# Strassen's seven products for the down projection of a retention and feed-forward kernel

## Chip, cores and metric

The kernel runs on one core of a Trainium2 chip. The metric is the device time of one execution in microseconds (us), the median of several runs.

## What is computed

The reference is a retention layer (attention without softmax, with a decay by distance) followed by a feed-forward layer with a sigmoid gelu. Cut to what matters:

```python
scores = scale * np.matmul(q, k.transpose(0, 1, 3, 2))      # 8 batches, 8 heads, 576 positions, 64 wide
Dmat = np.where(rel >= 0, gamma[:, None, None] ** rel[None, :, :], 0.0)
attn = np.matmul(scores * Dmat[None], v)
x = attn.transpose(0, 2, 1, 3).reshape(4608, 512)
h = x @ w_in                                                # 512 x 2048
g = h * (1.0 / (1.0 + np.exp(-1.702 * h)))
out = g @ w_out                                             # 2048 x 512, float32
```

## The kernel before

**Units and chunks.** The 4608 tokens are 36 units of 128 (NU). Of each nine units, four belong to one batch, four to the next, and the ninth holds the last 64 positions of both ("the third kind": units 8, 17, 26, 35). Four units make a chunk, 0 to 8 (NCH = 9). The hidden width of 2048 is 16 slices f of 128 (NF).

**Feed-forward of a chunk.** In the up phase, `up(c, f)` (L552) makes four 512-wide matmuls into bank psA or psB, by turns with f, and ScalarE writes gelu of that bank into gT (L561). Chunk 1 uses `up_group` (L565) instead: two slices f of half the tokens, 256 columns each. In the down phase, `down(c, r, s, b)` (L580) makes four 512-wide matmuls for unit r over slices 4s to 4s+3, and after s = 3 `finish_unit` copies the bank to osb on ScalarE (L592) and stores it from SP's queue (L598). psA and psB change with r. Chunk 8 takes its units as 3, 0, 1 and then 2 in two column parts.

**Attention of a pair of units.** `block(j)` (L642) treats units 2j and 2j+1. On TensorE: `inter` (L466, reads the cast states kv and the transposed queries), `values` (L512, reads the masked scores pm and the scaled vp), and between its two phases `ahead(j + 1)` (L620), the scores (L491) and state updates (L419) of the next pair. On VectorE: `x_out_pair` (L540) writes the input xT of the feed-forward; then, by `ahead_out(j + 1)` (L627), `scores_out` (L504) twice and `state_sum` (L432) four times, two for a pair with a unit of the third kind. On ScalarE: `state_cast` (L444), which turns the new states into bf16 for the next block's `inter`. The arguments `nxt` and `cast` leave out the next pair's part, or put the cast elsewhere and the sums ahead of the scores.

**Order.** The order of each engine's instructions is written out by hand: every call of `op` appends to its engine's stream, and waits are worked out from the names read and written. An engine runs its stream in that order, and an instruction that waits holds up all that stand behind it on its engine. In a chunk c of 2 to 7, blocks 2c+2 and 2c+3 stand in the down phase, behind (r, s) = (0, 0) and (2, 0). Chunk 1 has block 3 in its up phase, without the next pair's part, and blocks 4 and 5 in its down phase. `scale_v(m)` (L343, vp from the loaded v) stands at f = 0, 4, 8, 12 of the up phase. At the top of a chunk stand the DMA transposes of four units on SP (L389) and the loads of four later units on POOL (L660), which wait for those transposes.

**Chunk 0** has PE transposes, copies and blocks of its own between its matmuls; `load_wout` (L267) brings w_out in four parts. Before the first data are there, `warm` matmuls run on a zeroed part of gT.

Of the kernel before, what the change touches and what calls it, by code (L numbers as in the profile page):

```python
# [160 lines left out]
def bass_retnet_parallel__then__act_gelu_quick_kernel(  # L161
# [10 lines left out]
    with es:  # L172
# [10 lines left out]
        osb = [sb(f"osb{i}", [P, DM], FP32) for i in range(4)]  # L183
# [6 lines left out]
        gT = [sb(f"gT{i}", [P, NF, 512], BF16) for i in range(2)]  # L190
# [17 lines left out]
        op = pr.op  # L208

# [34 lines left out]
        def load_kq0(which):  # L244
            src = (k, q)[which]
            op("sp", lambda e: e.dma_start(
                osb[1 + which].ap().rearrange("p (h d) -> p h d", d=DH),
                src[0, :, 0:P, :].rearrange("h p d -> p h d")),
               writes=[f"osb{1 + which}_0"], dma=f"d_kq0f_{which}")

        def cast_kq0(which, eng):
            dst, src = kqn[0][:, which, :, :], osb[1 + which].ap().rearrange("p (h d) -> p h d", d=DH)
            if eng == "act":
                op("act", lambda e: e.activation(dst, src, AF.Copy),
                   reads=[f"osb{1 + which}_0"], writes=[f"kq0_{which}"])
            else:
                op("dve", lambda e: e.tensor_copy(dst, src),
                   reads=[f"osb{1 + which}_0"], writes=[f"kq0_{which}"])
# [293 lines left out]
        def up(c, f, lo=0, hi=4, b=None):  # L552
            b = b or "AB"[f % 2]
            n0, n1 = P * lo, P * hi
            for a in range(4):
# [6 lines left out]
                gT[c % 2][:, f, n0:n1], bank[b][:, n0:n1], AF.Gelu_apprx_sigmoid),  # L562
               reads=[b], writes=[f"g{c % 2}_{f}_{j}" for j in range(lo, hi)])

        def up_group(c, f0, nf, lo, hi, b):  # L565
            n = P * (hi - lo)
            for i in range(nf):
# [8 lines left out]
                gT[c % 2][:, f0 : f0 + nf, P * lo : P * hi],  # L576
                bank[b][:, 0 : n * nf].rearrange("p (f t) -> p f t", f=nf), AF.Gelu_apprx_sigmoid),
               reads=[b], writes=[f"g{c % 2}_{f}_{j}" for f in range(f0, f0 + nf) for j in range(lo, hi)])

        def down(c, r, s, b, n0=0, n1=DM):  # L580
            for f in range(4 * s, 4 * s + 4):
                op("pe", lambda e, f=f: e.matmul(  # L582
                    bank[b][:, 0 : n1 - n0], gT[c % 2][:, f, P * r : P * r + P], w_out_sb[:, f, n0:n1],
                    start=(f == 0), stop=(f == NF - 1)),
                   reads=[f"g{c % 2}_{f}_{r}", f"wout{f // 4}"], writes=[b])

        def down_out(c, r, b, n0=0, n1=DM, cp="act", eng="sp"):
            u = 4 * c + r
            i = u % 4
            src, dst = bank[b][:, 0 : n1 - n0], osb[i][:, n0:n1]  # L590
            if cp == "act":
                op("act", lambda e: e.activation(dst, src, AF.Copy), reads=[b], writes=[f"osb{i}_{n0}"])  # L592
            else:
                op("dve", lambda e: e.tensor_copy(dst, src), reads=[b], writes=[f"osb{i}_{n0}"])

            def f(e):
                return [
                    e.dma_start(out[S * bb + s0 : S * bb + s0 + n, n0:n1], osb[i][p0 : p0 + n, n0:n1])  # L598
                    for p0, n, bb, s0 in unit_rows(u)
                ]  # L600
            return op(eng, f, reads=[f"osb{i}_{n0}"], writes=[f"out{u}_{n0}"],
                      dma=f"d_o{i}_{n0}", ndma=len(unit_rows(u)))
# [24 lines left out]
        def ahead_out(j, cast=True):  # L627
            if 2 * j >= NU:
                return
            if cast:  # L630
                scores_out(2 * j, 2, 0)
                scores_out(2 * j, 2, 1)
            for u in (2 * j, 2 * j + 1):
                for a in range(2):
                    state_sum(u, a)
            if not cast:
                scores_out(2 * j, 2, 0)
                scores_out(2 * j, 2, 1)
            if cast:
                state_cast(2 * j, 2 * j + 2)  # L640

        def block(j, nxt=None, cast=True):  # L642
            started.clear()
# [11 lines left out]
            for hh in range(2):  # L655
                x_out_pair(j, hh)
            if nxt is None:
                ahead_out(j + 1, cast)
# [7 lines left out]
        last_store = {}  # L666

        def finish_unit(c, r, b, **kw):
            o = down_out(c, r, b, **kw)
            last_store[o.dma] = o  # L670

        def warm(n, b='A', w=512):
            for i in range(n):
                op("pe", lambda e: e.matmul(
                    bank[b][:, 0:w], gT[1][:, 0, 0:P], gT[1][:, 0, 0:w], skip_group_check=True),
                   reads=["warm"], writes=[b])

        def warm_quads(n):
            for i in range(n):
                r, c = i % 2, (i // 2) % 2  # L680
                op("pe", lambda e, r=r, c=c: e.matmul(
                    bank["AX"[r]][64 * c : 64 * c + 64, 0:64], gT[1][64 * r : 64 * r + 64, 0, 0:64],
                    gT[1][64 * r : 64 * r + 64, 0, 0:64], skip_group_check=True),
                   reads=["warm"], writes=["AX"[r]])

        def gelu_table():
            op("act", lambda e: e.activation(gT[1][:, 1, 0:4], gT[1][:, 0, 0:4], AF.Gelu_apprx_sigmoid),
               reads=["warm"], writes=["gelu_table"])

        def lead_in():  # L690
# [18 lines left out]
            op("dve", lambda e: e.memset(gT[1][:, 0, :], 0.0), writes=["warm"])  # L709
# [75 lines left out]
            def ahead45():  # L785
# [12 lines left out]
                (3, 1): lambda: block(2, lambda: None),  # L798
# [3 lines left out]
            for r, s in [(i % 2, i // 2) for i in range(8)] + [(i // 4, i % 4) for i in range(8, NF)]:  # L802
                down(0, r, s, "AB"[r % 2])
                if (r, s) in work:
                    work[r, s]()
                if s == 3:
                    finish_unit(0, r, "AB"[r % 2])

        def steady():
            for c in range(1, NCH):  # L810
# [8 lines left out]
                for u in range(4 * c + 10, 4 * c + 14):  # L819
                    load(u, after=[f"T{(4 * c + 9) % NQT}_0"])  # L820
                if c == 1:
                    for i in range(16):
                        f0, lo = 2 * (i % 8), 2 * (i // 8)
                        up_group(1, f0, 2, lo, lo + 2, "AB"[i % 2])
                        if i == 0:
                            ahead(3)
                            ahead_out(3, False)
# [4 lines left out]
                        if i == 5:  # L832
                            block(3, lambda: None)
                            scale_v(8)
                            scale_v(9)
                        if i == 8:
                            scale_v(10)
                            scale_v(11)
                else:
                    for f in range(NF):  # L840
# [3 lines left out]
                        if f % 4 == 0:  # L844
                            m = 4 * c + 6 + f // 4
                            if m < NU:
                                scale_v(m)
                if c == NCH - 1:
                    for r in (3, 0, 1):
                        b = "AB"[(r + 1) % 2]  # L850
# [87 lines left out]
```

## Time and profile before

| what | value |
|---|---|
| median of 3 runs | 295.31 us (295.15 to 295.53) |
| profiled execution, span | 293.4 us |
| VectorE busy | 99.7 us, 202 instructions |
| ScalarE busy | 133.7 us, 235 instructions |
| up phase of chunk 3 | 112.09 to 125.91 us |
| down phase of chunk 3, two blocks in it | 125.91 to 142.27 us |
| gelu of 128x512 (L561) | 597 ns, 120 times |
| copy of 128x512 out of a bank (L592) | 584 to 596 ns |
| scores_out of 128x512 (L506) | 679 to 680 ns |
| state_sum of 128x256 (L441) | 419 to 424 ns |
| state_cast of 128x1024 / 128x512 (L450) | 1057 / 627 ns |

All times are of one profiled execution, in microseconds from the start of its span. The median of the runs is of other executions, and also holds what lies around the span: 295.31 - 293.4 = 1.9 us. A matmul's own duration in the profile contains its way through the array; for the pace of a row of them, the step from one to the next is what counts, as the chain gives it. Engines are named PE (TensorE, with PEld for its weight loads), DVE (VectorE), ACT (ScalarE), POOL (GpSimd) and SP (SyncE).

### The profile page before, as it was taken

The page shows a single profiled execution, that of the slowest core. Times are in us where ns is not written, and L with a number is a line of the kernel's source. Part 1 is how long each engine was busy: PE and PEld are TensorE (multiplying, and loading weights), DVE is VectorE, ACT ScalarE, POOL GpSimd, SP SyncE. Part 2 cuts the span into 40 slices and gives each one's busy share as a digit, 9 for nine tenths or more (in the row PEclk, how much of TensorE's full clock was granted, in tenths as well). Part 3 has the DMA queues.
Part 4 walks back from the last instruction along what each step waited for, and adds up shares of the span by engine and source line. Part 5 has one row for each costly group of instructions (what it writes and reads, how often), then busy time and mean ns, then how long its engine had stood idle before and what let it go on. Part 6 is the DMA issues. An engine that isn't in the chain of part 4 may idle for free.

```text
span 293.4 us, 8059 instructions
## 1 busy us (share of the span) xinstructions
PE 287.7 (98%) x3650; PEld 141.2 (48%) x3650; DVE 99.7 (34%) x202; ACT 133.7 (46%) x235; POOL 110.2 (38%) x141
## 2 busy tenths in 40 slices
PE   8899999999999999999999999999999999999996
PEld 6575456775533553345334533454344434443344
DVE  5861056615650652054404360237013700410000
ACT  7466234661366135712672256324642365216611
POOL 9999798000960590292049103910170000000000
PEclk9999999999999999999999999999999999999999
DMA  9999999998999899799479935992692050111022
GB/s 172 175 211 206 209 231 249 235 120 213 125 236 115 98 230 227 93 161 200 133 106 153 188 108 113 178 182 80 137 142 71 20 131 2 38 72 38 0 65 78
DMA packets 116786, 40.63 MB, mean 139 GB/s; under 512 B 104080, under 2 KB 109968, under 8 KB 116752
## 3 DMA queue, kind: packets, MB, share of 16 engines
q0 software_dynamic: 79712, 22.82, 68.0%
q1 hardware_dynamic: 36896, 17.24, 24.8%
q8 instruction: 28, 0.46, 0.7%
q10 hardware_dynamic: 144, 0.07, 0.1%
q14 instruction: 6, 0.05, 0.0%
HBM read 36.70 MB, written 9.44 MB: 157 GB/s over the span
## 4 chain that ended last, share of the span: by engine, by line
PE 96%; DMA 2%; DVE 1%; issue 0%; ACT 0%; POOL 0%; POOLq 0%
PE psA L582 22%; PE psB L582 21%; PE psA L556 18%; PE psB L556 18%; PE psB L570 4%; PE psA L570 3%; DMA vn<-in_v_dram 2%; PE psX L481 2%; PE psC L497 1%; PE psY L519 1%; PE psX L519 1%; PE psK L426 1%; PE psD L497 1%; PE psE L426 1%; PE psK L403 1%; PE psE L361 0%
## 5 line engine op out<-in xcount | busy, mean ns | idle before, releaser
L226 POOL DMA_DIRECT2D kqn<-in_k_dram x39 | 35.1, 910 | 106.9 <-DMA kqT<-kqn 104.9
L582 PE MATMUL psA<-w_out_sb,gT 128*128 128x512 bf16 (+1 forms) x304 | 69.4, 371 | 0.3 <-issue 0.3
L582 PE MATMUL psB<-w_out_sb,gT 128*128 128x512 bf16 (+1 forms) x288 | 65.4, 376 | 0.0
L556 PE MATMUL psA<-xT,w_in_sb 128*128 128x512 bf16 x240 | 61.6, 379 | 0.0
L556 PE MATMUL psB<-xT,w_in_sb 128*128 128x512 bf16 x240 | 61.6, 379 | 0.0
L544 DVE TENSOR_TENSOR xT<-psX,gq 128x512 bf16<-128x512 f32 x16 | 11.1, 691 | 109.3 <-PE psX L519 109.3
L450 ACT ACTIVATE kv<-stm 128x1024 bf16<-128x1024 f32 (+1 forms) x18 | 15.6, 866 | 68.7 <-DVE stm L441 68.7
L582 PEld LDWEIGHTS psB<-w_out_sb,gT 128*128 128x128 bf16 x288 | 27.8, 98 | 32.5 <-ACT gT L561 0.3
L561 ACT ACTIVATE gT<-psB 128x512 bf16<-128x512 f32 x60 | 35.8, 597 | 15.8 <-PE psB L556 15.7
L561 ACT ACTIVATE gT<-psA 128x512 bf16<-128x512 f32 x60 | 35.8, 597 | 15.6 <-PE psA L556 15.6
L582 PEld LDWEIGHTS psA<-w_out_sb,gT 128*128 128x128 bf16 x304 | 27.2, 98 | 31.9 <-ACT gT L561 2.5
L239 POOL DMA_DIRECT2D vn<-in_v_dram x40 | 37.1, 942 | 0.1
L556 PEld LDWEIGHTS psA<-xT,w_in_sb 128*128 128x128 bf16 x240 | 19.2, 97 | 32.7 <-ACT gT L561 16.6
L556 PEld LDWEIGHTS psB<-xT,w_in_sb 128*128 128x128 bf16 x240 | 18.8, 97 | 33.0 <-ACT gT L561 16.4
L345 DVE TENSOR_TENSOR vp<-vn,vfac 128x512 bf16<-128x512 f32 x36 | 23.4, 684 | 30.8 <-DMA vn<-in_v_dram 30.8
L226 POOL DMA_DIRECT2D kqn<-in_q_dram x37 | 33.4, 917 | 0.6 <-issue 0.6
L592 ACT ACTIVATE osb<-psB 128x512 f32<-128x512 f32 (+1 forms) x18 | 10.6, 590 | 22.7 <-PE psB L582 22.5
L592 ACT ACTIVATE osb<-psA 128x512 f32<-128x512 f32 x18 | 10.5, 584 | 15.3 <-PE psA L582 15.3
L506 DVE TENSOR_TENSOR pm<-psC,mask 128x512 bf16<-128x512 f32 (+1 forms) x20 | 12.6, 628 | 8.7 <-PE psD L497 8.7
L506 DVE TENSOR_TENSOR pm<-psD,mask 128x512 bf16<-128x512 f32 (+1 forms) x20 | 12.5, 626 | 0.0
L570 PE MATMUL psB<-xT,w_in_sb 128*128 128x256 bf16 x96 | 12.5, 273 | 0.0
L441 DVE TENSOR_TENSOR stm<-psE,stm 128x256 f32<-128x256 f32 x28 | 11.9, 424 | 1.2
(86 smaller groups left out, 257.3 us busy)
## 6 DMA issues: line engine op xcount, KB each, us to landing
vn<-in_v_dram POOLq DMA_DIRECT2D x32, 256.0 KB, 5.6
out_dram<-osb SPq DMA_DIRECT2D x31, 256.0 KB, 2.6
kqn<-in_k_dram POOLq DMA_DIRECT2D x31, 128.0 KB, 5.5
kqn<-in_q_dram POOLq DMA_DIRECT2D x31, 128.0 KB, 5.7
w_out_sb<-in_moe_w_out_dram POOLq DMA_DIRECT2D x4, 512.0 KB, 13.3
w_in_sb<-in_moe_w_in_dram POOLq DMA_DIRECT2D x8, 128.0 KB, 5.0
w_in_sb<-in_moe_w_in_dram POOLq DMA_DIRECT2D x4, 256.0 KB, 7.2
vn<-in_v_dram POOLq DMA_DIRECT2D x8, 128.0 KB, 7.0
```

Source lines behind the costliest of these rows:

```text
L226: e.dma_start(kqn[sl][p0 : p0 + n, which, :, :], src[b, :, s0 : s0 + n, :].rearrange("h p d -> p h d"),)
L239: e.dma_start(vn[sl][p0 : p0 + n, :, :], v[b, :, s0 : s0 + n, :].rearrange("h p d -> p h d"))
L345: op(eng, lambda e: e.tensor_tensor(vp[u % NVP].ap(), vn[sl].ap(), vfac[:, ty, :, None].to_broadcast([P, H, DH]), ALU.mult), reads=[f"vn{s ...
L441: op("dve", lambda e: e.tensor_tensor(dst, src, prev, ALU.add), reads=[KB[a], f"stm{(i - 1) % 8}"], writes=[f"stm{i % 8}"])
L450: op("act", lambda e: e.activation(kv[:, i0 % NKV : i0 % NKV + n, :, :], stm[:, i0 % 8 : i0 % 8 + n, :, :], AF.Copy), reads=[f"stm{(i0 + i ...
L506: op("dve", lambda e: e.tensor_tensor(pm[(u0 // 2) % 2][hh][:, c0:c1].rearrange("p (a i) -> p a i", i=64), ps32(SB[hh])[:, c0:c1].rearrang ...
L544: op("dve", lambda e: e.tensor_tensor(xT[ch % 2][:, slice(hh, 4, 2), P * jj : P * jj + 2 * P].rearrange("p g (u t) -> p u g t", u=2), ps32 ...
L556: op("pe", lambda e, a=a: e.matmul(bank[b][:, n0:n1], w_in_sb[:, a, P * f : P * f + P], xT[c % 2][:, a, n0:n1], start=(a == 0), stop=(a == ...
L561: op("act", lambda e: e.activation(gT[c % 2][:, f, n0:n1], bank[b][:, n0:n1], AF.Gelu_apprx_sigmoid), reads=[b], writes=[f"g{c % 2}_{f}_{j ...
L570: op("pe", lambda e, a=a, f=f, i=i: e.matmul(bank[b][:, n * i : n * i + n], w_in_sb[:, a, P * f : P * f + P], xT[c % 2][:, a, P * lo : P * ...
L582: op("pe", lambda e, f=f: e.matmul(bank[b][:, 0 : n1 - n0], gT[c % 2][:, f, P * r : P * r + P], w_out_sb[:, f, n0:n1], start=(f == 0), sto ...
L592: op("act", lambda e: e.activation(dst, src, AF.Copy), reads=[b], writes=[f"osb{i}_{n0}"])
```

## The change

The down projection of two pairs of units is taken as a 2 x 2 block product. Rows 0 and 1 are two groups of units (0, 1 and 2, 3), the inner index is split into even and odd slices f, and the columns of w_out into two halves of 256. Seven products of 256 columns (`Pair.run`) take the place of eight. Three of them have sums of gT blocks as the left operand, and two have differences, which overwrite the block in gT (`Pair.sums`, five VectorE instructions for f 0 to 7 and five for f 8 to 15). Five have sums of w_out blocks as the right operand (`wsums`, 20 VectorE instructions in chunk 0's down phase). The products alternate between psA and psB; three of them add onto what the bank holds. ScalarE copies a bank out three times per chunk, and VectorE combines six times (`comb`), two of these without a bank. Chunk 0 keeps the old form. Chunk 8 takes units 3 and 0 by Strassen with one unit per row, and then units 1 and 2 in the old form.

In chunks 2 to 7, block 2c+2 goes into the up phase, behind f = 9 (f = 14 in chunk 2), at once with all its parts. Block 2c+3 stays in the down phase: its TensorE part runs at hook 2, and the rest is given out two calls to a hook. `scale_v` stands at f = 0, 2, 4, 6. gT has one buffer in place of two, and osb is one tensor.

```diff
-        osb = [sb(f"osb{i}", [P, DM], FP32) for i in range(4)]
+        osb = sb("osb", [P, 4, DM], FP32)
...
-        gT = [sb(f"gT{i}", [P, NF, 512], BF16) for i in range(2)]
+        gT = sb("gT", [P, NF, 512], BF16)
+        gsum = sb("gsum", [P, 3, NF // 2, 256], BF16)
+        wsum = sb("wsum", [P, 5, NF // 2, 256], BF16)
+        wtmp = sb("wtmp", [P, 512], FP32)
+        warmt = sb("warmt", [P, 512], BF16)
+        tblt = sb("tblt", [P, 4], BF16)
...
+        def wsums(i):
+            def part(r, c):
+                return w_out_sb[:, 4 * i + r : 4 * i + 4 : 2, 256 * c : 256 * c + 256]
+            for n, (x, y, alu) in enumerate((
+                ((0, 0), (1, 1), ALU.add), ((0, 0), (0, 1), ALU.add), ((1, 0), (1, 1), ALU.add),
+                ((0, 1), (1, 1), ALU.subtract), ((1, 0), (0, 0), ALU.subtract),
+            )):
+                op("dve", lambda e, n=n, x=x, y=y, alu=alu: e.tensor_tensor(
+                    wsum[:, n, 2 * i : 2 * i + 2, :], part(*x), part(*y), alu),
+                   reads=[f"wout{i}"], writes=[f"ws{n}_{i}"])
...
+        class Pair:
+            def __init__(self, r0, r1, nt):
+                self.r, self.nt, self.n = (r0, r1), nt, P * nt
+            def gpart(self, row, col, f0, f1):
+                t0 = P * self.r[row]
+                return gT[:, f0 + col : f1 : 2, t0 : t0 + self.n]
+            def gkeys(self, row, col, f0, f1):
+                return [f"g_{f}_{j}" for f in range(f0 + col, f1, 2)
+                        for j in range(self.r[row], self.r[row] + self.nt)]
+            def sums(self, f0, f1):
+                a, g = (lambda r, c: self.gpart(r, c, f0, f1)), (lambda r, c: self.gkeys(r, c, f0, f1))
+                for n, x, y in ((1, (1, 0), (1, 1)), (2, (0, 0), (0, 1)), (0, (0, 0), (1, 1))):
+                    op("dve", lambda e, n=n, x=x, y=y: e.tensor_tensor(
+                        gsum[:, n, f0 // 2 : f1 // 2, 0 : self.n], a(*x), a(*y), ALU.add),
+                       reads=g(*x) + g(*y), writes=[f"gs{n}_{k}" for k in range(f0 // 2, f1 // 2)])
+                for x, y in (((1, 0), (0, 0)), ((0, 1), (1, 1))):
+                    op("dve", lambda e, x=x, y=y: e.tensor_tensor(a(*x), a(*x), a(*y), ALU.subtract),
+                       reads=g(*x) + g(*y), writes=g(*x))
...
+            def product(self, b, left, right, more=False):
+                for t in range(self.nt):
+                    for k in range(NF // 2):
+                        (x, kx), (y, ky) = left(k, t), right(k)
+                        op("pe", lambda e, x=x, y=y, t=t, s=not more and t == 0 and k == 0, z=k == NF // 2 - 1: e.matmul(
+                            bank[b][:, 256 * t : 256 * t + 256], x, y, start=s, stop=z, skip_group_check=True),
+                           reads=[kx, ky], writes=[b])
...
+            def run(self, c, hook):
+                q, A, B, W = self.quarter, self.bank("A"), self.bank("B"), self.tmp()
+                add, sub = ALU.add, ALU.subtract
+                self.product("A", self.raw(1, 1), wsummed(4))
+                self.copy(q(1, 1), A)
+                hook(0)
+                self.product("B", self.raw(0, 0), wsummed(3))
+                self.comb(W, B, q(1, 1), add)
+                hook(1)
+                self.product("A", self.summed(1), wpart(0, 0), True)
+                self.copy(q(1, 0), A)
+                hook(2)
+                self.comb(q(1, 1), W, q(1, 0), sub)
+                self.product("B", self.summed(2), wpart(1, 1), True)
+                self.copy(q(0, 1), B)
+                hook(3)
+                self.comb(q(0, 0), W, q(0, 1), sub)
+                self.product("A", self.summed(0), wsummed(0))
+                self.comb(q(1, 1), A, q(1, 1), add)
+                hook(4)
+                self.product("B", self.raw(1, 0), wsummed(1))
+                self.comb(q(1, 1), B, q(1, 1), add)
+                for j in range(self.nt):
+                    store(4 * c + self.r[1] + j)
+                hook(5)
+                self.product("A", self.raw(0, 1), wsummed(2), True)
+                self.comb(q(0, 0), A, q(0, 0), add)
+                for j in range(self.nt):
+                    store(4 * c + self.r[0] + j)
+                hook(6)
...
         def ahead_out(j, cast=True):
             if 2 * j >= NU:
-                return
-            if cast:
-                scores_out(2 * j, 2, 0)
-                scores_out(2 * j, 2, 1)
-            for u in (2 * j, 2 * j + 1):
-                for a in range(2):
-                    state_sum(u, a)
-            if not cast:
-                scores_out(2 * j, 2, 0)
-                scores_out(2 * j, 2, 1)
-            if cast:
-                state_cast(2 * j, 2 * j + 2)
+                return []
+            sc = [lambda hh=hh: scores_out(2 * j, 2, hh) for hh in range(2)]
+            st = [lambda u=u, a=a: state_sum(u, a) for u in (2 * j, 2 * j + 1) for a in range(2)]
+            return sc + st + [lambda: state_cast(2 * j, 2 * j + 2)] if cast else st + sc
...
-            for hh in range(2):
-                x_out_pair(j, hh)
-            if nxt is None:
-                ahead_out(j + 1, cast)
+            rest = [lambda hh=hh: x_out_pair(j, hh) for hh in range(2)]
+            return rest + (ahead_out(j + 1, cast) if nxt is None else [])
+        def now(rest):
+            for f in rest:
+                f()
...
+                if r == 1:
+                    wsums(s)
...
+            four = Pair(0, 2, 2)
...
+                        if i in (11, 15):
+                            four.sums(2 * (i - 11), 2 * (i - 11) + 8)
                 else:
+                    pair = Pair(3, 0, 1) if last else four
                     for f in range(NF):
                         up(c, f)
                         if c == 2 and f in (1, 3):
                             state_cast(12 + f // 2, 13 + f // 2)
-                        if f % 4 == 0:
-                            m = 4 * c + 6 + f // 4
+                        if f in (0, 2, 4, 6):
+                            m = 4 * c + 6 + f // 2
                             if m < NU:
                                 scale_v(m)
-                if c == NCH - 1:
-                    for r in (3, 0, 1):
-                        b = "AB"[(r + 1) % 2]
+                        if f in (7, 15):
+                            pair.sums(f - 7, f + 1)
+                        if f == (14 if c == 2 else 9) and not last:
+                            now(block(2 * c + 2))
+                if last:
+                    pair.run(c, lambda i: None)
+                    for n0, n1, b, cp in ((0, 512, "B", "act"),):
                         for s in range(4):
-                            down(c, r, s, b)
-                        finish_unit(c, r, b)
-                    for n0, n1, b, cp in ((0, 384, "B", "act"), (384, 512, "A", "dve")):
+                            down(c, 1, s, b, n0, n1)
+                        finish_unit(c, 1, b)
+                    for n0, n1, b, cp in ((0, 384, "A", "act"), (384, 512, "B", "dve")):
                         for s in range(4):
                             down(c, 2, s, b, n0, n1)
                         finish_unit(c, 2, b, n0=n0, n1=n1, cp=cp, eng="sp" if n0 == 0 else "act")
                     break
-                for r in range(4):
-                    for s in range(4):
-                        down(c, r, s, "AB"[r % 2])
-                        if c == 1 and r == 1 and s == 0:
-                            scale_v(12)
-                            scale_v(13)
-                        if c == 1 and (r, s) == (0, 2):
+                rest = []
+                def hook(i):
+                    if c == 1:
+                        if i == 0:
                             ahead(4)
-                            ahead_out(4)
-                        if (r, s) in (((1, 2), (3, 0)) if c == 1 else ((0, 0), (2, 0))):
-                            j = 2 * c + 2 + (r >= 2)
-                            if 2 * j < NU:
-                                block(j, cast=c != 1)
-                    finish_unit(c, r, "AB"[r % 2])
-                    if c == 1 and r == 1:
-                        state_cast(10, 12)
+                            rest.extend(ahead_out(4))
+                        if i == 1:
+                            rest.extend([lambda: scale_v(12), lambda: scale_v(13)])
+                        if i == 2:
+                            now(rest)
+                            rest.clear()
+                            rest.extend(block(4, cast=False))
+                        if i == 4:
+                            now(rest)
+                            rest.clear()
+                            state_cast(10, 12)
+                        if i == 5:
+                            rest.extend(block(5, cast=False))
+                    elif i == 2 and 2 * (2 * c + 3) < NU:
+                        rest.extend(block(2 * c + 3))
+                    n = len(rest) if i == 6 else 2
+                    now(rest[:n])
+                    del rest[:n]
+                four.run(c, hook)
 ```

## The prediction

> **What bounds the kernel now.** I read the page first, then the chain that ended last in order of time, then the timelines of ScalarE and VectorE over one down phase (the chunk whose down phase starts at 95.87 us), then the groups by line with shapes kept apart.
>
> ```profile
> span 293.4 us, 8059 instructions
> PE 287.7 (98%) x3650; PEld 141.2 (48%) x3650; DVE 99.7 (34%) x202; ACT 133.7 (46%) x235; POOL 110.2 (38%) x141
> PE 96%; DMA 2%; DVE 1%; issue 0%; ACT 0%; POOL 0%; POOLq 0%
> ```
>
> TensorE is busy 98% of the span and is 96% of the chain; the others are below half. So TensorE's own work is the bound, and whatever makes it wait is added in full. Its rates and its steps, from the chain in order of time (start, length, what):
>
> ```profile
> 58.76 0.87 PE psB L570 x8
> ...
> 95.87 0.86 PE psA L582 x4
> 97.86 2.70 PE psA L582 x12
> 100.56 3.45 PE psB L582 x16
> ...
> 112.09 0.86 PE psA L556 x4
> ```
>
> Sixteen 512-wide matmuls take 3.45 us: 216 ns each. Eight 256-wide ones, each with a new stationary operand, take 0.87 us: 109 ns each. The hole from 95.87 + 0.86 = 96.73 to 97.86 is one attention block on TensorE, 1.13 us. A bank is written again 0.86 us after its last matmul in the up phase, and nothing waits. What ScalarE and VectorE do behind that block, from their timelines:
>
> ```profile
> 97.93 0.69 DVE L544 TENSOR_TENSOR xT<-psX,gq 128x512 bf16<-128x512 f32 x1 [1.18 <-PE psX L519]
> 98.54 0.68 DVE L544 TENSOR_TENSOR xT<-psY,gq 128x512 bf16<-128x512 f32 x1
> ...
> 101.70 0.42 DVE L441 TENSOR_TENSOR stm<-psE,stm 128x256 f32<-128x256 f32 x1
> ```
>
> ```profile
> 95.91 0.60 ACT L561 ACTIVATE gT<-psB 128x512 bf16<-128x512 f32 x1 [0.27 <-PE psB L556]
> 102.16 1.06 ACT L450 ACTIVATE kv<-stm 128x1024 bf16<-128x1024 f32 x1 [5.65 <-DVE stm L441]
> 103.12 0.58 ACT L592 ACTIVATE osb<-psA 128x512 f32<-128x512 f32 x1
> ```
>
> VectorE needs 4.2 us after the block (two x_out and two scores_out 0.60 apart, four state_sum 0.46 apart), and ScalarE stands still 5.65 us before the state cast that closes it. From the block's end (97.86) to the first ScalarE instruction behind the cast (103.12) pass 5.26 us. In the down phase that is free: the copy behind the cast frees psA, which TensorE wants again only after 2.70 + 3.45 = 6.15 us of matmuls.
>
> **The change, part by part.**
>
> *Fewer matmuls.* A chunk's down phase has 64 x 216 ns = 13.82 us. Seven products of 2 x 8 matmuls of 256 columns are 112 x 108.75 ns = 12.18 us: -1.64 us, in chunks 1 to 7: -11.5. In chunk 8, two units go from 32 x 216 ns to 56 x 108.75 ns: -0.8. Together **-12.3 us**.
>
> *The moved block (chunks 3 to 7).* Its TensorE work, 1.13 us, only moves. But block(2c+2) now runs behind up(9) with everything it appends: on VectorE two x_out, two scores_out and four state_sum; on ScalarE the state cast, which stands ahead of gelu(10). No DMA moves with it. Its transposes stay on SP's queue ahead of the chunk, and POOL's loads stay where they were. Count from the end of up(7). Gelu(7) is done at 0.65, and VectorE starts the five sums of f 0..7 at 0.72. They are 1024-element bf16 instructions from SBUF, which no row shows. These rows bound them:
>
> ```profile
> L441 DVE TENSOR_TENSOR stm<-psE,stm 128x256 f32<-128x256 f32 x28 | 11.9, 424 | 1.2
> L544 DVE TENSOR_TENSOR xT<-psX,gq 128x512 bf16<-128x512 f32 x16 | 11.1, 691 | 109.3 <-PE psX L519 109.3
> L377 DVE COPY kqT<-psE 128x512 bf16<-128x512 bf16 x5 | 2.1, 422 | 2.1 <-PE psE L361 2.0
> L439 DVE COPY stm<-psK 128x256 f32<-128x256 f32 x7 | 2.9, 414 | 0.7 <-PE psE L426 0.7
> ```
>
> With f32 in it, 256 more elements cost 691 - 424 = 267 ns, so 1024 would be 1.22 us, 1.13 apart. A copy of 512 bf16 elements costs what one of 256 f32 does, half as much per element: 1024 bf16 would then cost what 512 f32 do, 0.69 us, 0.60 apart. I take 0.60, since the bf16 row is nearest in type, and keep 1.13 for the range.
>
> The sums then end at 3.72. The block ends on TensorE at 1.73 (up 8 and 9) + 1.13 = 2.86, so its VectorE chain starts at 3.72, not at 2.93, and ends 4.23 later at 7.95. The cast runs then, gelu(10) starts 0.96 later at 8.91 and ends at 9.51. TensorE has up(10) in psA and up(11) in psB meanwhile, to 2.86 + 1.73 = 4.59. Up(12) needs psA, which gelu(10) has not read, and so starts at 9.55: **a wait of 4.9 us**. Chunks 5 and 7 prepare a unit of the third kind (units 26 and 35), with two state_sum fewer (0.92) and a cast half as wide (1057 against 627 ns): 3.6. Together 3 x 4.9 + 2 x 3.6 = **+21.9 us**.
>
> *Chunk 2* has its block behind up(14), and scale_v(17) now stands at f = 6, ahead of the sums. Before, that instruction waited for its load:
>
> ```profile
> 96.06 0.69 DVE L345 TENSOR_TENSOR vp<-vn,vfac 128x512 bf16<-128x512 f32 x1 [7.51 <-DMA vn<-in_v_dram]
> ```
>
> I keep 96.06, as POOL issues that load early in chunk 1's down phase. With the terms below, up(2) starts at about 83.6 (81.92 before), so the block is over at 97.7 and up(15) at 98.6. VectorE is free at 96.7, does five sums to 99.7 and the block's chain to 103.95. The cast ends at 104.9 and gelu(15) at 105.5. The first product reads f = 15 with its eighth matmul, at 99.3, so it waits **6.2 us**. Had the load landed long before, the wait would be 4.3.
>
> *The last recombination.* The seventh product ends in psA, and up(0) of the next chunk writes psA. VectorE must read it first: 0.07 to start (97.86 to 97.93), 0.69, and as much as 0.05 back: 0.8 us in each of chunks 1 to 7, **+5.6**. Before, the last copy read psB while up(0) wrote psA. The other recombinations are hidden by the products beside them: each bank rests for a whole product, 1.74 us, and a read takes 0.69 (VectorE) or 0.60 (ScalarE). If VectorE is behind by more than a microsecond there, that cover is gone.
>
> *Chunk 1.* Blocks 4 and 5 come closer to the work that feeds them. Behind the five sums (0.72 to 3.72), scores_out and the recombination, the state sums of unit 9 end at 6.5 and their cast at 7.15. Block 4 is reached at 5.6, with 0.2 us of work that needs no cast: a wait of 1.3. The cast for block 5 ends at 14.3; TensorE gets there at 13.3: 1.0. Together **+2.3**.
>
> *Chunk 0* gains 20 sums of w_out: 512 bf16 elements each, about 0.36 apart by the rows above. Fifteen fit where VectorE idles (14.66 us ahead of 37.98). Five stand between the transposed copies of units 4 and 5: 1.8 us less the 0.89 idle there, of which TensorE feels **+0.7**.
>
> *Chunk 8*: its fourth product waits for the recombination behind five sums of half size, **+0.35**. Three output copies on ScalarE in place of four, the stores (SP, behind them) and the single gT buffer cost nothing: ScalarE is idle half of the down phase, and gelu of the next chunk waits for matmuls that are behind the readers in TensorE's order anyway.
>
> *The clock.* TensorE would stand still 3.6 to 6.2 us six times. The longest hole now is 0.84 us, near 8 us, and the matmuls after it are no slower. At the start, the first 512-wide matmuls took up to 634 ns against 379 later, though the granted clock reads 1.00; that stretch, 1.2 to about 6.4 us, ran at half rate and lost 2.6 us. So a stall costs between 0 and 2.6 more. I take 0.7, nearer the hole of known length: **+4.2** (0 to 15.6).
>
> The Trainium skill has a rule against the change here (TensorE: Matmul & The Clock Gate, "HAM oscillation"): TensorE idle for a window of some 3.4 us falls to half clock and needs a busy window to recover. No run here shows it; by it each stall longer than the window could add about 1.7 us, an estimate from that page's window, and the sum would end some 6 us above the one without a clock term.
>
> **Sum**: -12.3 + 21.9 + 6.2 + 5.6 + 2.3 + 0.7 + 0.35 + 4.2 = +28.9 on the span of 293.4, that is 322.3. The median of the runs is 295.31, 1.9 above the span: **324.2**.
>
> **Rivals.**
>
> *The cast holds nobody up (faster).* If gelu(10) were through before up(12) wants psA, as the down phase manages with its 6.15 us of cover, the moved blocks would cost nothing in chunks 2 to 7. Left are -12.3 + 5.6 + 2.3 + 0.7 + 0.35 = -3.3: 292.0. The change decides for this side once block end to gelu(10)'s end takes under 1.73 us; the row says 5.26 + 0.60. For it speaks only that TensorE has that much less to do. 5%.
>
> *VectorE adds bf16 at the f32 rate.* Five sums take 2.65 us longer. The up-phase waits grow by 2.65 in five chunks (13.2) and chunk 2's by as much; in seven down phases the recombination W is late by about 1.1 (7.7): +23.6, or 348. The f32 rows speak for it, the bf16 copy against. 9%. The skill's VectorE: DVE Perf Modes, "The perf-mode tier table", has this sum at double rate, which would leave the forecast as it is.
>
> *The clock takes its full price*, 15.6 in place of 4.2: 336. 11%.
>
> *Strassen saves no TensorE time*, because 256-wide matmuls with a weight load each run slower than 109 ns. L570 does just that at 109 ns, so I give it 1% (about 336, no saving).
>
> **Numbers.** The forecast, slower through waits on ScalarE's queue, has 74%, and its own range is 310 to 333: without the clock term and with VectorE done before the block ends (0.8 us less in five chunks), 316; some 6 less if the loads land early and the small terms are nothing. To 340 the clock rival is in, the f32-rate rival out. What this kernel's measurement can tell from no change is about 0.2%. Faster 0.05, within it 0.01, slower 0.94.
>
> **What would show it.** Right: ScalarE's cast in the up phase with 4 to 6 us of idle "DVE stm" ahead of it, and TensorE holes of 3.6 to 5 us in front of an up matmul into psA in chunks 3 to 7, released by ScalarE's gT. The sums should take 0.69 us, the products 1.74 us each, and each chunk should show a hole of 0.8 us at up(0) behind VectorE. Wrong: no such holes; sums of 1.2 us; matmuls of 512 columns above 379 ns after holes (then the clock term is too small); chunk 2's scale_v(17) not waiting.

## The result, and the profile after

The changed kernel takes 331.81 us (median; 331.45 to 332.31), the kernel before 295.27 us. The ratio is 1.123, 95% interval [1.122, 1.125]: slower by 36.5 us. Forecast were 324, with a range of 310 to 340.

From the page of the changed kernel: the span, the busy time of each engine, the clock granted to TensorE in 40 slices, and the chain that ended last by engine.

```profile
span 329.7 us, 8931 instructions
PE 291.8 (89%) x4010; PEld 181.5 (55%) x4010; DVE 181.6 (55%) x350; ACT 129.5 (39%) x229; POOL 110.1 (33%) x141
PEclk9999999999997899899987999799978999799999
PE 60%; DVE 14%; POOL 14%; DMA 5%; ACT 4%; issue 2%; SPq 0%; POOLq 0%
```

TensorE fell from 98% busy to 89%, though it had an eighth less to do in the down phases of chunks 1 to 7. VectorE's busy time rose by 82 us, to 55% of the span. The clock, which was full in every slice before, dips once in each of chunks 2 to 7. What TensorE waited for, longest first (total, times, longest):

```profile
PE psA L564 <- ACT gT L569: 21.1, 5, 4.7
PE psA L564 <- DVE osb L692: 5.5, 7, 0.8
PE psA L673 <- ACT gT L569: 4.2, 1, 4.2
PE psX L489 <- ACT kv L458: 1.7, 2, 1.0
```

L564 is the matmul of the up phase, L569 its gelu, L673 a product, L692 a recombination, L458 the state cast. The first line is the five waits in the up phases of chunks 3 to 7, the third is chunk 2's, and the second is the recombination (VectorE combining a product's bank with earlier results) ahead of each up(0). The fourth is the two waits for casts in chunk 1.

One of the five, in chunk 3: ScalarE's timeline, then TensorE's (start, length, instructions, and in brackets the idle time before them and what ended it).

```profile
129.44 0.60 ACT L569 ACTIVATE gT<-psB 128x512 bf16<-128x512 f32 x1 [0.27 <-PE psB L564]
135.57 1.06 ACT L458 ACTIVATE kv<-stm 128x1024 bf16<-128x1024 f32 x1 [5.54 <-DVE stm L449]
136.54 0.58 ACT L569 ACTIVATE gT<-psA 128x512 bf16<-128x512 f32 x1
```

```profile
131.41 1.03 PE L564 MATMUL psB<-xT,w_in_sb 128*128 128x512 bf16 x4
137.17 1.89 PE L564 MATMUL psA<-xT,w_in_sb 128*128 128x512 bf16 x4 [4.73 <-ACT gT L569]
138.85 1.80 PE L564 MATMUL psB<-xT,w_in_sb 128*128 128x512 bf16 x4
140.49 1.03 PE L564 MATMUL psA<-xT,w_in_sb 128*128 128x512 bf16 x4
```

ScalarE has finished gelu(9) at 130.0 and stands still for 5.54 us in front of the cast, which waits for VectorE's last state_sum. Gelu(10), whose bank was full at about 131.6, starts at 136.54. TensorE, out of banks after up(11), starts up(12) at 137.17. Then something more is seen: four matmuls that take 1.03 us elsewhere take 1.89 and 1.80.

A down phase, by the chain in order of time (chunk 3; the first and the last product, and up(0) of chunk 4):

```profile
142.38 1.85 PE psA L673 x16
144.23 1.75 PE psB L673 x16
...
154.20 1.76 PE psA L673 x16
156.73 1.04 PE psA L564 x4
```

The products run at the counted pace, 1.75 us for 16 matmuls. From 155.96 to 156.73 there is the hole at the last recombination, 0.77 us.

### The profile page after: what moved, and what is told of

Same layout as the page of the kernel before. It is cut to its first block, busy times and chain, and to the rows that moved or that the text cites. A ratio compares the mean times of both kernels' runs of the same rounds, so it can differ in the third digit from the quotient of the medians.

```text
span 329.7 us, 8931 instructions
## 1 busy us (share of the span) xinstructions
PE 291.8 (89%) x4010; PEld 181.5 (55%) x4010; DVE 181.6 (55%) x350; ACT 129.5 (39%) x229; POOL 110.1 (33%) x141
## 4 chain that ended last, share of the span: by engine, by line
PE 60%; DVE 14%; POOL 14%; DMA 5%; ACT 4%; issue 2%; SPq 0%; POOLq 0%
PE psA L673 15%; PE psA L564 14%; PE psB L564 13%; PE psB L673 12%; POOL kqn L234 7%; DMA vn<-in_v_dram 4%; POOL vn L247 4%; DVE gsum L653 3%; DVE stm L449 2%; POOL w_in_sb L269 2%; DVE xT L552 2%; DVE pm L514 2%; DVE gT L657 2%; ACT gT L569 2%; ACT kv L458 2%
## 5 line engine op out<-in xcount | busy, mean ns | idle before, releaser
L564 PE MATMUL psA<-xT,w_in_sb 128*128 128x512 bf16 x240 | 67.4, 407 | 26.6 <-ACT gT L569 21.1
L653 DVE TENSOR_TENSOR gsum<-gT 128x1024 bf16<-128x1024 bf16 (+1 forms) x48 | 28.7, 654 | 84.2 <-ACT gT L569 81.5
L564 PE MATMUL psB<-xT,w_in_sb 128*128 128x512 bf16 x240 | 65.8, 399 | 0.0
L564 PEld LDWEIGHTS psA<-xT,w_in_sb 128*128 128x128 bf16 x240 | 20.3, 103 | 62.2 <-ACT gT L569 35.5
L569 ACT ACTIVATE gT<-psA 128x512 bf16<-128x512 f32 x60 | 35.7, 595 | 38.3 <-PE psA L564 38.3
L569 ACT ACTIVATE gT<-psB 128x512 bf16<-128x512 f32 x60 | 35.8, 596 | 18.2 <-PE psB L564 18.1
L564 PEld LDWEIGHTS psB<-xT,w_in_sb 128*128 128x128 bf16 x240 | 21.3, 102 | 34.8 <-ACT gT L569 12.2
L458 ACT ACTIVATE kv<-stm 128x1024 bf16<-128x1024 f32 (+1 forms) x18 | 15.6, 865 | 56.7 <-DVE stm L449 56.7
L673 PE MATMUL psA<-wsum,gT 128*128 128x256 bf16 x240 | 30.6, 278 | 4.2 <-ACT gT L569 4.2
L673 PE MATMUL psB<-wsum,gT 128*128 128x256 bf16 x240 | 30.5, 282 | 0.0
L673 PEld LDWEIGHTS psA<-wsum,gT 128*128 128x128 bf16 x240 | 22.7, 99 | 10.8 <-ACT gT L569 7.5
L673 PEld LDWEIGHTS psB<-wsum,gT 128*128 128x128 bf16 x240 | 24.3, 101 | 3.5
L353 DVE TENSOR_TENSOR vp<-vn,vfac 128x512 bf16<-128x512 f32 x36 | 23.1, 684 | 5.4 <-DMA vn<-in_v_dram 5.4
L552 DVE TENSOR_TENSOR xT<-psX,gq 128x512 bf16<-128x512 f32 x16 | 11.0, 689 | 22.1 <-PE psX L527 22.1
L689 ACT ACTIVATE osb<-psA 128x512 f32<-128x512 f32 (+1 forms) x16 | 9.1, 570 | 34.6 <-PE psA L673 34.6
L657 DVE TENSOR_TENSOR gT<-gT 128x1024 bf16<-128x1024 bf16 (+1 forms) x32 | 19.5, 651 | 0.0
L673 PE MATMUL psB<-w_out_sb,gsum 128*128 128x256 bf16 x120 | 14.5, 273 | 0.1
L673 PE MATMUL psA<-w_out_sb,gsum 128*128 128x256 bf16 x120 | 14.4, 273 | 0.0
L673 PE MATMUL psA<-wsum,gsum 128*128 128x256 bf16 x120 | 14.4, 273 | 0.0
```

The costliest lines, as they stand in the source:

```text
L353: op(eng, lambda e: e.tensor_tensor(vp[u % NVP].ap(), vn[sl].ap(), vfac[:, ty, :, None].to_broadcast([P, H, DH]), ALU.mult), reads=[f"vn{s ...
L458: op("act", lambda e: e.activation(kv[:, i0 % NKV : i0 % NKV + n, :, :], stm[:, i0 % 8 : i0 % 8 + n, :, :], AF.Copy), reads=[f"stm{(i0 + i ...
L552: op("dve", lambda e: e.tensor_tensor(xT[ch % 2][:, slice(hh, 4, 2), P * jj : P * jj + 2 * P].rearrange("p g (u t) -> p u g t", u=2), ps32 ...
L564: op("pe", lambda e, a=a: e.matmul(bank[b][:, n0:n1], w_in_sb[:, a, P * f : P * f + P], xT[c % 2][:, a, n0:n1], start=(a == 0), stop=(a == ...
L569: op("act", lambda e: e.activation(gT[:, f, n0:n1], bank[b][:, n0:n1], AF.Gelu_apprx_sigmoid), reads=[b], writes=[f"g_{f}_{j}" for j in ra ...
L653: op("dve", lambda e, n=n, x=x, y=y: e.tensor_tensor(gsum[:, n, f0 // 2 : f1 // 2, 0 : self.n], a(*x), a(*y), ALU.add), reads=g(*x) + g(*y ...
```

## The experiments

Three theories were put against each other. **Q**: the cast stands in ScalarE's queue ahead of gelu(10), TensorE runs out of banks, and the clock falls behind each wait. **V**: TensorE waits because VectorE has 82 us of new work. **S**: the 256-wide products are what slows TensorE and its clock.

**The cast alone moved back.** `e1_cast_late`:

```diff
 if f == (14 if c == 2 else 9) and not last:
-    now(block(2 * c + 2))
+    held = block(2 * c + 2)
+    now(held[:-1])          # all but the state cast
+    held = held[-1:]
...
 def hook(i):
+    if c > 1 and i == 0:
+        now(held)
```

> The changed kernel, but the state cast of the block in the up phase is issued at hook 0 of the down phase (behind ScalarE's first copy); everything else of that block stays where it is. Theory Q (the cast stands ahead of gelu(10) on ScalarE, TensorE waits for gelu, and the clock drops after each wait): the 21.1 + 4.2 us of waiting for gelu go, and with them the slow matmuls behind each wait (13.1 us by the chain of the changed kernel); 331.8 - 38.4 = 293, between 291 and 297, granted clock 1.00. Rival V (TensorE waits because VectorE has 82 us of new work): VectorE's work is the same, so TensorE waits for it elsewhere; 320 or more. Rival S (the 256-wide products themselves bring the clock down): the waits go, the clock stays near 0.95; about 306.

Measured: 294.85 us, ratio to before 0.999 [0.998, 1.000]. No wait of TensorE for gelu is left among its waits, and no dip of the clock from chunk 1 on. One ScalarE instruction per chunk, issued later, gives back 37 us, with VectorE's work unchanged: V and S fall.

**The move alone.** `e2_move_only`, on the kernel before:

```diff
 for f in range(NF):
     up(c, f)
...
+    if f == (14 if c == 2 else 9) and c < NCH - 1:
+        block(2 * c + 2)
...
-    if (r, s) in (((1, 2), (3, 0)) if c == 1 else ((0, 0), (2, 0))):
+    if (r, s) in (((1, 2), (3, 0)) if c == 1 else ((2, 0),)):
```

> The kernel before with one thing of the change alone: block 2c+2 in the up phase (behind f = 9, in chunk 2 behind f = 14) with its cast in place; no Strassen, no sums. Q: VectorE's chain starts when the block ends, so the waits are 4.1 us in chunks 3, 4, 6, 2.8 in 5 and 7, 1.7 in chunk 2, together 19.6; the clock adds some 1.8 to 2.5 behind the four longest; 295.3 + 19.6 + 8 = 323, between 315 and 328. V: no VectorE work is added, so within 2 us of before, 293 to 298. S: as V, and the clock at 1.00.

Measured: 326.35 us, ratio 1.102 [1.095, 1.109]. Its two largest waits of TensorE:

```profile
PE psA L556 <- ACT gT L561: 17.2, 5, 4.0
PE psA L582 <- ACT gT L561: 1.7, 1, 1.7
```

Expected were 17.9 and 1.7. So a kernel with no Strassen in it loses 31.3 us (326.35 - 295.04, the kernel before run beside it) in the same way; in the changed kernel the place of the cast was worth 37.0.

**Strassen without the move.** `e3_both_down`:

```diff
-if f == (14 if c == 2 else 9) and not last:
-    now(block(2 * c + 2))
...
-elif i == 2 and 2 * (2 * c + 3) < NU:
-    rest.extend(block(2 * c + 3))
-n = len(rest) if i == 6 else 2
+elif i in (0, 4):
+    rest.extend(block(2 * c + 2 + i // 4))
+n = len(rest) if i in ((3, 6) if c > 1 else (6,)) else 2
```

> The changed kernel with block 2c+2 back in the down phase (at hook 0, block 2c+3 at hook 4, their parts given out by the hooks): Strassen without the move. Q: no cast stands ahead of a gelu; the clock stays at 1.00. VectorE has about 15.4 us of work in a down phase of 14.4, so up to some 1.5 us per chunk are lost: 290 to 303. V: 320 or more, as all of VectorE's new work is there and even crowded into the down phase. S: clock near 0.95, about 306.

Measured: 301.94 us, ratio 1.023 [1.021, 1.025], clock 1.00: in Q's interval, at its upper end, but not as Q had it, which said that no cast would stand ahead of a gelu. With two blocks and seven products in one phase, the cast of the second block comes so late that it does stand ahead of the next chunk's gelu. ScalarE's timeline at the start of chunk 4, and TensorE's two largest waits:

```profile
147.32 1.06 ACT L458 ACTIVATE kv<-stm 128x1024 bf16<-128x1024 f32 x1 [7.37 <-DVE stm L449]
148.28 0.58 ACT L569 ACTIVATE gT<-psA 128x512 bf16<-128x512 f32 x1
```

```profile
PE psA L564 <- DVE osb L692: 7.3, 7, 1.1
PE psA L564 <- ACT gT L569: 5.5, 4, 1.4
```

(The first of the two lines reads longer than the 5.5 of the changed kernel because this profile lacks the record of the first matmul behind each of these waits, 0.22 us.) So in this arrangement Strassen gains nothing with both blocks beside it, while `e1_cast_late`, with one block taken out of the down phase, is 7.1 us faster (301.94 - 294.85). It is the place of the cast that costs, and not the move as such: `e1_cast_late` has the same move, and no wait for gelu.

**The wait in steps.** The cast behind gelu(10), gelu(11) or gelu(12), chunk 2's at hook 0. The diff is that of `e1_cast_late` with

```diff
+if c > 2 and f == 10 and not last:   # 11, 12
+    now(held)
+    held = []
```

> As e1_cast_late, but in chunks 3 to 7 the cast stands behind gelu(10), one slice later than in the changed kernel (chunk 2 keeps it at hook 0). Q: TensorE has one up slice (0.86 us) more to do before it needs a bank, so the waits are 3.9 us in chunks 3, 4 and 6 and 2.6 in 5 and 7, 17 us in all over e1_cast_late's 294.9, and the clock adds 1.8 to 2.5 behind each: 319 to 324 if the 2.6 us waits drop the clock too (as one of 2.7 us in e2_move_only did), 316 to 319 if only those above 3.4 us do. V: no change from the changed kernel, 332.

> The cast behind gelu(11). Q: waits of 3.0 us in chunks 3, 4, 6 and 1.7 in 5 and 7, 12.4 us in all: 307 without any drop of the clock (if it takes an idle time above 3.4 us), 312 to 315 if the 3.0 us waits drop it, 316 to 318 if the 1.7 us ones do too. V: 332.

> The cast behind gelu(12). Q: waits of 2.1 us in chunks 3, 4, 6 and 0.8 in 5 and 7, 8 us in all: 303 without a drop of the clock, 307 to 310 if an idle time of 2.1 us drops it. V: 332.

Measured: 320.30, 311.49 and 306.15 us. Each step gives TensorE one more up slice (0.86 us) before it lacks a bank. The waits in chunk 3 of the four profiles, from the changed kernel to d12, are 4.73, 3.88, 3.01 and 2.15 us: steps of 0.85 to 0.87. V, which expected 332 each time, is out. With the cast behind gelu(10), the time lies in the interval of the branch in which every wait drops the clock (319 to 324). The other two times lie between their branches (307 and 312 to 315; 303 and 307 to 310): some of their waits dropped the clock and some did not. How the clock answered is in the last section.

**The sums behind the block.** `e5_sums_behind`:

```diff
-if f in (7, 15):
-    pair.sums(f - 7, f + 1)
 if f == (14 if c == 2 else 9) and not last:
     now(block(2 * c + 2))
+if f in ((7, 15) if c == 2 or last else (9, 15)):
+    pair.sums(0 if f < 15 else 8, 8 if f < 15 else 16)
```

> The changed kernel with the cast in place, and in chunks 3 to 7 VectorE's five sums of f 0 to 7 behind the block's VectorE work in place of ahead of it. Q, with the sums as a small term: the block's chain starts when the block ends, 0.8 us (up to 0.9) earlier in five chunks: 331.8 - 4 = 328, between 326 and 329, with the clock dropping as before. V: the sums are what TensorE waits for, so most of the 21 us of waits go: below 316.

Measured: 327.00 us. The wait in chunk 3 is 4.06 in place of 4.73, in chunk 5 2.71 in place of 3.52. The sums delay the block's chain by 0.7 to 0.8 us, and that is all they do to these waits.

**More work for TensorE.** `e6_fill` puts 14 matmuls of zeros, whose result nobody reads, into the time in which TensorE waits:

```diff
+if f == (15 if c == 2 else 11) and not last:
+    warm(14, "X")
```

> The changed kernel with more work: 14 matmuls of 512 zeros into bank psX (free once VectorE has read it), in chunks 3 to 7 behind up(11) and in chunk 2 behind up(15), where TensorE has nothing to do until the cast is through; nothing else is changed, and nobody reads what they write. They take 14 x 0.216 = 3.0 us of waits of 3.5 to 4.7. If the slow matmuls behind the waits come from TensorE standing idle, the waits end when they did, the clock stays at 1.00, and the 13.1 us of slow stretches go: 331.8 - 13 = 319, between 317 and 322. If something else slows them (the restart behind a semaphore, the load of the other engines), 331 to 333.

Measured: 319.57 us, clock 1.00 throughout. (This trace holds no record of a change of the clock; the matmuls bear it out. From 7.5 us on none of them takes more than 391 ns, against 635 in the changed kernel.) The clock in chunk 3, in three stretches of the changed kernel and then in the first two of them for `e6_fill` (columns: stretch, its length, busy time and number of instructions of PE, PEld, DVE, ACT and POOL, granted clock, DMA share, GB/s):

```profile
132.20:137.10 4.90, 0.24 (x2) 0.00 (x0) 3.24 (x7) 1.53 (x3) 4.90 (x7) 0.99 1.70 176
137.10:140.50 3.40, 3.33 (x9) 1.20 (x10) 0.00 (x0) 1.10 (x3) 3.31 (x4) 0.51 1.73 196
140.50:142.30 1.80, 1.80 (x10) 0.69 (x9) 0.00 (x0) 1.19 (x2) 0.00 (x0) 1.00 2.01 184
```

```profile
132.20:137.10 4.90, 3.19 (x16) 1.20 (x14) 1.57 (x4) 2.55 (x4) 4.90 (x7) 1.00 1.75 196
137.10:140.50 3.40, 3.40 (x24) 1.84 (x23) 0.71 (x2) 1.86 (x4) 1.65 (x2) 1.00 1.85 209
```

In the changed kernel the clock reads 0.51 behind the wait and is full 3.4 us later. By the clock's records in the trace it stood at half from 137.00 to 140.41 us, so it fell while TensorE was still idle, 0.17 us before the wait ended at 137.17; in chunk 4 it fell at 171.13, 2.2 us before the end of the wait. And TensorE's timeline of `e6_fill` there:

```profile
130.60 3.19 PE L786 MATMUL psX<-warmt 128*128 128x512 bf16 x14
135.50 1.04 PE L564 MATMUL psA<-xT,w_in_sb 128*128 128x512 bf16 x4 [1.71 <-ACT gT L569]
136.37 1.03 PE L564 MATMUL psB<-xT,w_in_sb 128*128 128x512 bf16 x4
```

The wait for gelu still ends it, but the matmuls behind it run at full pace. Work that nobody needs makes the kernel 12.2 us faster (331.81 - 319.57): that is the price of the clock.

**A version that is faster than both.** `e4_cast_late_banks` is `e1_cast_late` with the banks exchanged in chunks 2, 4, 6 and 8, in the up phase, the products and chunk 8's end:

```diff
+def sw(c):
+    return c > 1 and c % 2 == 0
...
-    b = b or "AB"[f % 2]
+    b = b or "AB"[(f + sw(c)) % 2]
...
-    self.product("A", self.raw(1, 1), wsummed(4))
+    self.product("AB"[sw(c)], self.raw(1, 1), wsummed(4))
...
```

> e1_cast_late, and in even chunks from 2 on psA and psB change places in the up phase and the products, so that up(0) never writes the bank that VectorE's last recombination reads. Q, with the wait of 0.78 us per chunk as its own term: 5.5 us less than e1_cast_late, so 288, between 285 and 291; faster than before. V: no better than e1_cast_late. If the 0.78 us only hid another wait at the same place (the cast or the first gelu), less than 2 us are won.

Measured: 289.42 us, ratio to before 0.980 [0.978, 0.982]. No wait for "DVE osb" (L695 in this kernel) is left among TensorE's waits: the seven waits of the recombination were a term of their own, worth 5.4 us (294.85 - 289.42). It was run again, beside a variant with the last five sums of w_out at another place:

```diff
-if r == 1:
+if r == 1 and s < 3 or (r, s) == (3, 3):
     wsums(s)
```

> e4_cast_late_banks again beside e7_cast_late_banks_wsum, with more rounds: 289.4, between 288.5 and 290.

> e4_cast_late_banks, with the last five sums of w_out behind (r, s) = (3, 3) of chunk 0's down phase, where no transposed copy waits behind them. If chunk 0 loses 0.7 us through these five, 0.7 less than e4_cast_late_banks run beside it; if not, within 0.3.

Measured: 288.76 us (ratio 0.978 [0.975, 0.980]) for the former and 288.79 for the latter. The place of the five sums makes no difference that can be told.

## Why the prediction was right, and which term was too small

The sign, the mechanism and its place were as forecast. Term by term, in us (the first row is worked out from the measured pace of the products, the others are waits or differences in time that were read off):

| term | forecast | measured | where |
|---|---|---|---|
| fewer matmul columns | -12.3 | -11.8 | products at 1.75, not 1.74: 49 x 0.01 less is won |
| waits in the up phases of chunks 3 to 7 | +21.9 | +21.1 | waits of TensorE |
| chunk 2 | +6.2 | +4.2 | the same |
| last recombination | +5.6 | +5.5 | the same; 5.4 by e4_cast_late_banks |
| chunk 1 | +2.3 | +1.7 | the same (kv) |
| chunk 0 | +0.7 | +0.4 | see below |
| chunk 8 | +0.35 | +0.4 | wait for VectorE's wtmp, in the list of waits by weight loads (PEld) |
| the clock | +4.2 | +12.2 | e6_fill |
| sum | +28.9 | +33.7 | the spans differ by 36.3 |

**The clock** is the term that was mis-sized. I took 0.7 us for each of six waits, nearer a hole of 0.84 us that did nothing than the start of the kernel, which lost 2.6. Measured are 12.2 / 6 = 2.0 each. The sum of the stretches in which the changed kernel's clock stood at half, six in all, gives the same (they are listed in the last section):

```profile
sum 30.71, PE 24.57 PEld 10.67 DVE 4.01 ACT 11.99 POOL 18.34; mean PE 4.10 PEld 1.78 DVE 0.67 ACT 2.00 POOL 3.06
```

TensorE worked in 24.57 us of these, and at half rate half of that is lost: 12.3. The bounds, 0 and 2.6, were right, the choice between them was not: a wait of 4 us should have been put with the long idle time. The sign that I had named for this, 512-wide matmuls above 379 ns behind the holes, is there. The rival "the clock takes its full price" was thus the better number (336). Taken with its 2.6 in place of 0.7, the forecast would have erred by 4 to the other side. That the sum came within 7.6 us (331.8 - 324.2) is in part luck: the clock was 8.0 too low, and the waits of chunks 1 to 7 and of chunk 0 together 3.8 too high. The rule of the Trainium skill that was weighed there (TensorE: Matmul & The Clock Gate, "HAM oscillation") names the mechanism, and the 1.7 us per stall that I estimated from its window is closer than my 0.7. But I added it up wrongly: six stalls at 1.7 are 10.2 us above the sum without a clock term; they are 6 above the sum that has my 4.2 in it.

**Chunk 2** was over-sized because its load landed earlier than I kept it. VectorE's timeline of the changed kernel:

```profile
90.87 0.69 DVE L353 TENSOR_TENSOR vp<-vn,vfac 128x512 bf16<-128x512 f32 x1 [2.17 <-DMA vn<-in_v_dram]
98.65 0.69 DVE L552 TENSOR_TENSOR xT<-psX,gq 128x512 bf16<-128x512 f32 x1 [3.48 <-PE psX L527]
```

Scale_v(17) ran at 90.87, not at 96.06, so VectorE was idle when the block ended and the wait was the 4.3 given for that case. A load's landing need not keep its time when the work around it moves.

**The sums** took 687 ns against the 691 that I took by the bf16 row, so the rival with the f32 rate falls, and the double rate that the prediction cites for them agrees. The recombinations from psA took 688 ns:

```profile
L653 DVE TENSOR_TENSOR gsum<-gT 128x1024 bf16<-128x1024 bf16 x42 | 26.5, 687 | 71.3 <-ACT gT L569 68.6 <-ACT gT L583 2.7
L692 DVE TENSOR_TENSOR osb<-psA,osb 128x512 f32<-128x512 f32 x14 | 9.6, 688 | 4.4 <-PE psA L673 4.4
```

**The faster rival** (292.0) was wrong for the kernel as changed, and its condition is what `e1_cast_late` brings about: with the cast out of gelu's way, 294.9. It was low by 2.9 us, and the table above leaves 36.3 - 33.7 = 2.6 without a row. Part of this is seen: the first product of each chunk takes 1.85 in place of 1.75, 0.1 in seven chunks, and a DMA transpose holds up scores in chunk 1 for 0.6. The rest stays open. In **chunk 0**, from the first matmul of the down phase to the second up group (psB) of chunk 1 are 19.31 us in the changed kernel and 18.91 before: 0.4. With the five sums elsewhere they are 19.15, against 19.31 in the run beside it, but the runs' times don't tell that apart.

## What to carry to other kernels

A block of work that ends in one instruction on a shared engine is safe only where that engine's next instruction is not urgent. Before moving a block, follow the last instruction of its chain on every engine, count from the block's end to the end of whatever is queued behind it, and compare that with the buffered work of the engine that bounds the kernel (here 5.9 us against two banks, 1.73 us). If it does not fit, leave the block where it is wanted and issue only its last instruction later. And where a saving ends in a bank, check who reads that bank before it is written again: the exchange of two names was worth 5.4 us here, nearly half of what Strassen's products save (11.8).

## What the runs showed of the hardware

TensorE's clock falls through idle times that are quite short. The waits of TensorE in up phases, and the four 512-wide matmuls after them (1.03 to 1.04 us at full clock, 1.89 in the slow stretch):

| wait, us | what followed |
|---|---|
| 3.5 to 4.7 (changed kernel, five) | 1.89 each time |
| 3.75 to 4.06 (d10, e5_sums_behind and e2_move_only, nine) | slow each time, in two of them from the second group on |
| 2.66 to 2.71 (d10, e5_sums_behind and e2_move_only, two each) | slow five times, in one of these from the second group on; full once |
| 3.01, 3.02, 2.89 (d11) | 1.78, 1.89, 1.04 |
| 2.15, 2.15, 2.02 (d12) | 1.84, 1.26 and then slow, 1.04 |
| 1.80 and 1.80 (d11) | 1.04, 1.04 |

From `d12`, TensorE's timeline: the same wait in chunks 3 and 4, and a slightly shorter one in chunk 6.

```profile
131.11 1.84 PE L564 MATMUL psB<-xT,w_in_sb 128*128 128x512 bf16 x4 [2.15 <-ACT gT L569]
164.65 1.26 PE L564 MATMUL psB<-xT,w_in_sb 128*128 128x512 bf16 x4 [2.15 <-ACT gT L569]
165.70 3.40 PE L673 MATMUL psA<-wsum,gT 128*128 128x256 bf16 x16
228.68 1.04 PE L564 MATMUL psB<-xT,w_in_sb 128*128 128x512 bf16 x4 [2.02 <-ACT gT L569]
```

So every wait of 3.5 us and more brought the clock down, between 2.0 and 3.1 most did and some did not, and none up to 1.8 did; 16 matmuls of 256 columns then took 3.40 us in place of 1.9 to 2.0.

Why nearly equal waits end differently can be seen from the clock's records in the traces. In each profile the changes lie on a grid of its own: from one to the next are 3.41 us or a whole multiple of that (in the changed kernel the clock is at half from 102.87 to 109.69, 137.00 to 140.41, 171.13 to 177.96, 208.68 to 212.09, 242.81 to 249.64 and 280.36 to 283.77). The falls go with the time that TensorE stood idle between two ticks of the grid. In all profiles together, the clock fell at the end of each of the 24 stretches at full clock with 2.15 us or more without a matmul, of two of the ten with 1.57 to 2.05 us, and of none with less. (Where a matmul's record is missing, the idle time reads up to some 0.2 us too long.) Two such stretches and those behind them, first from `d12` in chunk 3, where the wait of 2.15 us lies within one, then from `d11` in chunk 6, where a tick parts the longer wait of 2.89 us into 1.81 and 1.08 (columns as above; the clock is the third number from the end):

```profile
127.79:131.20 3.41, 1.26 (x7) 0.40 (x6) 1.59 (x4) 1.77 (x4) 3.41 (x5) 1.00 1.66 204
131.20:134.61 3.41, 3.41 (x13) 1.85 (x14) 0.99 (x2) 0.94 (x2) 3.15 (x4) 0.50 1.75 196
```

```profile
226.74:230.15 3.41, 1.60 (x8) 0.44 (x6) 2.79 (x7) 1.03 (x2) 3.41 (x6) 1.00 1.56 161
230.15:233.57 3.42, 2.34 (x14) 1.26 (x15) 0.00 (x0) 2.51 (x5) 0.27 (x1) 1.00 0.65 102
```

The four executions of `d11` took 309.12 to 312.86 us, at mean clocks of 0.994 to 0.984, as fits a grid that lies differently each time; what sets the grid, no run here shows. The rule of the Trainium skill named above (TensorE: Matmul & The Clock Gate, "HAM oscillation") warns of idle times above some 3.4 us. The 3.41 us of the grid agree with that length, but the waits of 2.15 and 2.7 us that brought the clock down are shorter, and the measurement decides.
